# Remainder differences made once on the compact channels and transposed by DMA, in place of subtractions of transposed remainder tiles, together with a new order of the work

## Chip, cores, metric

The kernel runs on one core of a Trainium2 chip. The metric is the device time of one execution in microseconds (us), lower is better. A profiled execution has its own "span", the time from the first to the last instruction, some 2 us shorter than the device time. All comparisons are between executions in the fast state, at a granted TensorE clock of 0.99 or more, but for one profile whose state is unknown, which is marked.

Engines are named as in the profile: PE is TensorE's matmuls, PEld its weight loads, DVE is VectorE, ACT is ScalarE, POOL is GpSimd, SP is SyncE. "L727" is a line of the kernel. The change moves the line numbers by two or so: the matmul helper is L727 before and L729 after.

## The reference

A causal convolution in time with 15 taps two steps apart, a gate, and a projection. x is (2, 16000, 144), w is (15, 144, 288), w_o is (144, 144), all bfloat16.

```python
h = sum over i of  xp[:, pad - 2*i : pad - 2*i + T, :] @ w[i]      # 15 taps, 288 columns
z = tanh(h[..., :144]) * sigmoid(h[..., 144:])
return z @ w_o
```

## The kernel before

The convolution isn't computed tap by tap. Time is dealt out in octets of eight steps to 128 rows, and a fast-convolution scheme builds sums of taps (weights) and differences of inputs (data). Fewer products are needed that way, and VectorE pays for it in subtractions. The 144 channels are split: 128 fill the contraction dimension of a matmul ("A": tiles XA, V, DU, DD, and GX, GV, GU, GD, which are differences of these), and the other 16 ("B", the remainder) are first packed, so that 8 time steps of 16 channels fill 128 rows.

B's way before the change: VectorE copies the 16 channels into XBc, four phases of time (step modulo 4). ScalarE copies a window of it into a staging tile STB, a DMA transposes STB into XB, and VectorE makes two difference tiles, BE and BF, from XB. The matmuls of one kind ("D groups") read BE and BF.

```python
def load_xb(o):                      # staging of the remainder of octet o
    ...
    for h in range(2):
        def cp(v, h=h):              # ScalarE, 4 blocks of 128 columns, 2 copies per octet
            src = bass.AP(XBc[:].tensor, (MB - 1 - m4 - h) * DB, [[4 * MB * DB, NP], [MB * DB, 4], [1, 128]])
            return v.activation(STB[:, q, 4 * h:4 * h + 4, :], src, ACT.Copy)
        g.add("act", cp, r=..., w=[("STB", q, h)], dur=0.5, prio=2, soft=gate[:1])
    g.add("sp", lambda e: e.dma_start_transpose(XB[:, s, :, :], STB[:, q, :, :]...), ...)

def b_diffs(o):                      # VectorE, 2 subtractions of 128x512 per octet, 30 octets
    s, p, q = bslot(o), bslot(o - 1), dslot(o)
    tt(ap(BE, 4 * q, [4]), ap(XB, 8 * s + 2, [(4, 2), 2]), ap(XB, 8 * s, [(4, 2), 2]), ...)
    tt(ap(BF, 4 * q, [4]), ap(XB, 8 * p + 6, ...), ap(XB, 8 * s, [(4, 2), 2]), ...)
```

STA and STB have two slots each (octet modulo 2), so a third octet's staging waits until the first one's transpose has landed.

The main loop runs 30 units. A unit is a list of items, given by a pattern string ("+" means that the item belongs to a later unit, so that work overlaps). The items that matter here: VE and VF make two partial sums in PSUM, the memory that TensorE writes its sums to; X0 and X1 make two more, which ScalarE copies to UX; the four D groups D11, D01, D00, D10 finish the four outputs; O items are the projection. VectorE adds the partial sums:

```python
PATTERN = "Y0a O2+ X0a+ O1+ Y0b X0b+ D11 D00 S0+ X1a+ D10 Y01 S1+ X1b+ D01 VE+ O0+ VF+"

# three per unit, "Xp sums" (Xp<-PS,UX, L1006): partial sum + UX into SBUF; a PSUM pair comes free
g.add("dve", ... wslot(wi), both(vb, 0, N2), UX[...], ALU.add ..., prio=1)
# three per unit, "PS+Xp sums" (PS<-PS,Xp, L1018): the Xp sum back into PSUM for D01, D00, D10
g.add("dve", ... both(d, 0, N2), src, wslot(wi), ALU.add ..., prio=0)
# one per unit, "PS+UX sum" (PS<-PS,UX, L1027): in place in PSUM, for D11
g.add("dve", ... both(vb, 0, N2), both(vb, 0, N2), UX[...], ALU.add ..., prio=0)
```

The order of every engine's instructions is fixed when the kernel is built. A list scheduler runs a rough model of the engines and always takes the instruction with the smallest `key = (st, op.prio, op.idx)`: earliest modelled start, then the lower priority number, then program order. Subtractions have priority 2. At run time each engine works its list off in that order.

## Time and profile before

The median was 327.86 us of three executions (327.82 to 328.47).

From the page of the kernel before: busy time of each engine (share of the span, number of instructions), the chain of waits by engine (the chain of work that ended last, followed back from the end), two groups of instructions (line, engine, operation, tiles, shape, count | busy us, mean ns | idle time before them and what ended it), and the remainder's transposes (count, median us from issue to landing).

```profile
PE 317.5 (97%) x2702; PEld 245.7 (75%) x2702; DVE 301.3 (92%) x659; ACT 261.5 (80%) x629; POOL 17.0 (5%) x29
...
PE 82%; DVE 13%; DMA 2%; ACT 1%; issue 1%; POOL 0%; POOLq 0%
...
L1006 DVE TENSOR_TENSOR Xp<-PS,UX 128x576 f32<-128x576 f32 x90 | 65.3, 752 | 6.4 <-PE PS L727 5.8
...
L655 ACT ACTIVATE STB<-XBc 128x512 bf16<-128x512 bf16 x60 | 35.7, 628 | 1.6 <-DVE XBc L535 1.1 <-DMA XB<-STB 0.4
...
XB<-STB SPq DMA_TRANSPOSE x30, 3.6
```

TensorE is the engine that ends last, 82% of the chain, and VectorE is nearly as busy. The Xp sums alone are 65.3 us of VectorE's time, with little idle time before them; the 60 BE and BF subtractions are 25 us of instruction time, 20 us from start to start.

A steady stretch of the kernel before, from the table by stretches (the columns are the stretch, its length, then busy us and instruction counts of PE, PEld, DVE, ACT, POOL, then the clock, the DMA share and GB/s):

```profile
120.00:160.00 40.00, 40.00 (x336) 30.69 (x335) 39.52 (x84) 34.16 (x84) 0.00 (x0) 1.00 0.76 163
```

VectorE works 39.52 of 40 us and TensorE starts 336 matmuls.

The largest wait of weight loads in the whole run before (engine, tile and line <- what ended the wait: us in total, times, longest):

```profile
PEld PS L727 <- DVE PS L1027: 5.0, 22, 0.2
```

It is one short wait in most units, for the PS+UX sum. Weight loads overlap matmuls, so only a part of it is lost time (1.94 of the 5.0 us, as worked out under the result).

VectorE's timeline in the kernel before, over part of one unit (start, duration, instruction; a note in brackets gives idle time before it, and its cause):

```profile
157.90 0.76 DVE L1006 TENSOR_TENSOR Xp<-PS,UX 128x576 f32<-128x576 f32 x1
158.57 0.30 DVE L756 TENSOR_TENSOR Z<-TS 128x288 bf16<-128x288 f16 x1
158.79 1.41 DVE L1006 TENSOR_TENSOR Xp<-PS,UX 128x576 f32<-128x576 f32 x2
160.12 0.68 DVE L673 TENSOR_TENSOR V<-XA 128x1024 bf16<-128x1024 bf16 x1
160.72 0.76 DVE L1027 TENSOR_TENSOR PS<-PS,UX 128x576 f32<-128x576 f32 x1
```

TensorE's weight loads in the kernel before at that moment:

```profile
161.53 0.24 PEld L727 LDWEIGHTS PS<-WA,DD 128*128 128x128 bf16 x3 [0.23 <-DVE PS L1027]
```

The PS+UX sum starts at 160.72. At 161.53 the first weight load of D11 (WA,DD) has waited for it.

### The profile page before, as it was taken

How to read it: one execution, taken by the hardware profiler on the slowest of the kernel's cores; microseconds unless marked ns; L12 is line 12 of the kernel's file. 1: busy time of each engine (PE TensorE's matmuls, PEld its weight loads, DVE VectorE, ACT ScalarE, POOL GpSimd, SP SyncE). 2: the span in 40 equal slices, each digit the busy share in tenths (PEclk: the TensorE clock that was granted, in tenths of full speed). 3: DMA queues.
4: the chain of work that ended last, by engine and by line, in shares of the span. 5: the costliest groups of instructions: out<-in, count | busy, mean ns of one | idle time of the engine just before them, and what ended most of it. 6: DMA issues, size and time to landing. Idle time of an engine off the chain costs nothing.

```text
span 325.7 us, 7051 instructions
## 1 busy us (share of the span) xinstructions
PE 317.5 (97%) x2702; PEld 245.7 (75%) x2702; DVE 301.3 (92%) x659; ACT 261.5 (80%) x629; POOL 17.0 (5%) x29
## 2 busy tenths in 40 slices
PE   7999999999999999999999999999999999999993
PEld 7877767777777777777777777777777777777773
DVE  1999999999999999999999999999999999895773
ACT  3657669889797988979798897979889797788774
POOL 8750000000000000000000000000000000000000
PEclk9999999999999999999999999999999999999998
DMA  8899975929386492939749193984929193321443
GB/s 211 275 115 241 178 161 51 247 49 203 114 175 174 93 239 49 201 117 177 174 91 254 35 192 125 121 228 84 252 47 205 39 183 93 74 73 38 109 111 109
DMA packets 112461, 46.46 MB, mean 143 GB/s; under 512 B 103774, under 2 KB 106255, under 8 KB 112429
## 3 DMA queue, kind: packets, MB, share of 16 engines
q1 hardware_dynamic: 111385, 45.54, 65.2%
q0 software_dynamic: 512, 0.33, 0.4%
q8 instruction: 21, 0.34, 0.4%
q10 hardware_dynamic: 532, 0.16, 0.2%
q14 instruction: 11, 0.09, 0.1%
HBM read 11.82 MB, written 9.22 MB: 65 GB/s over the span
## 4 chain that ended last, share of the span: by engine, by line
PE 82%; DVE 13%; DMA 2%; ACT 1%; issue 1%; POOL 0%; POOLq 0%
PE PS L727 72%; PE PS L826 8%; DVE Xp L1006 2%; DMA XA<-STA 2%; DVE V L673 2%; PE PS L541 1%; DVE PS L1018 1%; DVE DD L673 1%; DVE STA L636 1%; DVE DU L673 1%; DVE Z L756 1%; DVE GD L673 1%; DVE WC L616 1%; DVE GU L673 1%; DVE PS L1027 0%
## 5 line engine op out<-in xcount | busy, mean ns | idle before, releaser
L1006 DVE TENSOR_TENSOR Xp<-PS,UX 128x576 f32<-128x576 f32 x90 | 65.3, 752 | 6.4 <-PE PS L727 5.8
L1018 DVE TENSOR_TENSOR PS<-PS,Xp 128x576 f32<-128x576 f32 x90 | 68.2, 759 | 1.8 <-ACT OS L834 0.9
L727 PE MATMUL PS<-WA,GD 128*128 128x288 bf16 x360 | 69.8, 286 | 0.0
L748 ACT ACTIVATE TS<-PS 128x288 f16<-128x288 f32 x125 | 51.3, 410 | 17.0 <-PE PS L727 12.3
L885 ACT ACTIVATE PS<-PS 128x288 f32<-128x288 f32 x120 | 45.4, 402 | 16.1 <-PE PS L727 16.1
L751 ACT ACTIVATE TS<-PS 128x288 f16<-128x288 f32 x125 | 50.7, 406 | 0.0
L954 ACT ACTIVATE UX<-PS 128x576 f32<-128x576 f32 x60 | 39.0, 650 | 13.8 <-PE PS L727 12.5
L727 PE MATMUL PS<-WS,GU 128*128 128x288 bf16 x210 | 44.2, 286 | 0.0
L834 ACT ACTIVATE OS<-PS 128x432 bf16<-128x432 f32 (+1 forms) x88 | 42.4, 488 | 0.5
L826 PE MATMUL PS<-WOR,ZT 128*128 128x144 bf16 (+1 forms) x322 | 42.3, 253 | 0.0
L727 PEld LDWEIGHTS PS<-WA,GD 128*128 128x128 bf16 x360 | 34.1, 98 | 10.3 <-DVE PS L1018 0.6
L756 DVE TENSOR_TENSOR Z<-TS 128x288 bf16<-128x288 f16 x125 | 37.5, 301 | 3.9 <-ACT TS L751 3.8
L727 PE MATMUL PS<-WB,XB 128*128 128x288 bf16 x140 | 37.6, 286 | 0.0
L655 ACT ACTIVATE STB<-XBc 128x512 bf16<-128x512 bf16 x60 | 35.7, 628 | 1.6 <-DVE XBc L535 1.1
L727 PE MATMUL PS<-WB,BF 128*128 128x288 bf16 x120 | 34.3, 286 | 0.0
L727 PE MATMUL PS<-WB,BE 128*128 128x288 bf16 x120 | 34.3, 286 | 0.0
L826 PEld LDWEIGHTS PS<-WOR,ZT 128*128 128x128 bf16 x322 | 28.0, 98 | 6.1 <-ACT OS L834 0.6
L727 PE MATMUL PS<-WD,DD 128*128 128x288 bf16 x180 | 31.7, 286 | 0.3 <-ACT PS L885 0.2
L727 PE MATMUL PS<-WA,DD 128*128 128x288 bf16 x180 | 30.9, 287 | 0.0
L727 PE MATMUL PS<-WC,V 128*128 128x288 bf16 x180 | 30.6, 286 | 0.0
L727 PE MATMUL PS<-WT,DU 128*128 128x288 bf16 x120 | 24.8, 288 | 0.7 <-DVE Xp L1006 0.7
L727 PEld LDWEIGHTS PS<-WS,GU 128*128 128x128 bf16 x210 | 20.1, 98 | 6.1 <-ACT PS L885 0.6
(82 smaller groups left out, 513.2 us busy)
## 6 DMA issues: line engine op xcount, KB each, us to landing
Xr<-in_x_dram SPq DMA_DIRECT2D x15, 576.0 KB, 4.0
out_dram<-OS SPq DMA_DIRECT2D x30, 288.0 KB, 2.7
WA<-in_w_dram SPq DMA_DIRECT2D x3, 288.0 KB, 5.0
ZT<-Z SPq DMA_TRANSPOSE x32, 3.4
Xp<-in_x_dram SPq DMA_DIRECT2D x2, 252.0 KB, 4.8
XA<-STA SPq DMA_TRANSPOSE x30, 3.2
XB<-STB SPq DMA_TRANSPOSE x30, 3.6
Xp<-in_x_dram SPq DMA_DIRECT2D x1, 441.0 KB, 3.9
```

Of the source, the lines that this page charges most:

```text
L655: return v.activation(STB[:, q, 4 * h:4 * h + 4, :], src, ACT.Copy)
L673: return g.add("dve", lambda v: v.tensor_tensor(dst, a, b, ALU.subtract), r=r, w=wk, dur=t_tt(n), prio=prio, soft=gate[:1])
L727: return lambda t: t.matmul(bank(bk.b), lhsT=lhs(), rhs=rhs(), start=start, stop=True, skip_group_check=True)
L748: return a.activation(TS[:, s, 0, :, :], both(bk, 0, D), ACT.Tanh)
L751: return a.activation(TS[:, s, 1, :, :], both(bk, D, D), ACT.Sigmoid)
L756: return v.tensor_tensor(dst, TS[:, s, 0, :, :], TS[:, s, 1, :, :], ALU.mult)
L826: return t.matmul(PS[:, c0:c0 + n * D], lhsT=ZT[:, zt, blk, :], rhs=WOR[:, wi:wi + n, :].rearrange("p a b -> p (a b)"), start=first, stop= ...
L834: return e.tensor_copy(dst, src) if eng == "dve" else e.activation(dst, src, ACT.Copy)
L885: g.add("act", lambda e: e.activation(bank(bk.b + 1), bank(bk.b), ACT.Copy), w=[bk], dur=t_act(N2), prio=0)
L954: g.add("act", lambda e: e.activation(UX[:, k, u % NU, :, :], both(X, 0, N2), ACT.Copy), r=[X], w=[("UX", k, u % NU)], frees=[X], dur=t_ac ...
L1006: g.add("dve", lambda v, k=k, wi=wi, vb=vb, us=us: v.tensor_tensor(wslot(wi), both(vb, 0, N2), UX[:, k, us, :, :], ALU.add), r=[vb, ("UX", ...
L1018: return v.tensor_tensor(both(d, 0, N2), src, wslot(wi), ALU.add)
```

## The change

The difference of two time steps is the same whether it's taken before or after a transpose. The change takes it before: XBc grows to eight planes, VectorE subtracts once on the compact 16 channels (16 instructions in place of 60), and the differences travel through STB, the DMA and XB along with the sums' operands. STB and XB tiles grow from 8 to 12 blocks, so ScalarE copies and the DMA transposes half as much again. One difference has the opposite sign, hence a negated weight tile. Along with that, the XA tiles got 8 slots in place of 11, items were put in another order, the Xp sums got priority 0, staging is spread in smaller steps, and the last store goes out on SyncE's queue.

```diff
-    NA = 11
+    NA = 8
...
-    NB = 7
-    NBD = 4
+    NB = 6
-    PATTERNS = {29: "Y0a O2 O1 Y01 Y0b D11 D01 D00 D10 O0"}
-    SPREAS = 10
-    PATTERN = "Y0a O2+ X0a+ O1+ Y0b X0b+ D11 D00 S0+ X1a+ D10 Y01 S1+ X1b+ D01 VE+ O0+ VF+"
+    PATTERNS = {29: 'O2 O1 Y01 Y0a D11 O0 Y0b D01 D00 D10', 28: ..., 1: ..., 0: ..., 2: ...}
+    SPREAS = 9
+    PATTERN = "Y0a O2+ X0a+ O1+ Y0b X0b+ D11 D00 S0+ X1a+ D10 Y01 S1+ X1b+ D01 VE+ VF+ O0+"
...
-        XBc = sb("XBc", [NP, 4, MB, DB], BF16)
-        STB = sb("STB", [NP, NST, 8, 128], BF16)
-        XB = sb("XB", [NP, NB, 8, 128], BF16)
-        BE = sb("BE", [NP, NBD, 4, 128], BF16)
-        BF = sb("BF", [NP, NBD, 4, 128], BF16)
+        XBc = sb("XBc", [NP, 8, MB, DB], BF16)
+        STB = sb("STB", [NP, NST, 12, 128], BF16)
+        XB = sb("XB", [NP, NB, 12, 128], BF16)
...
+        def diff_b(eng, m0, nm, r, tag):
+            i0 = MB - m0 - nm
+            def f(v):
+                pat = lambda ph, grp: bass.AP(XBc[:].tensor, (ph * MB + i0) * DB, [[8 * MB * DB, NP], [grp, 2], [MB * DB, 2], [1, nm * DB]])
+                return v.tensor_tensor(pat(2, -2 * MB * DB), pat(6, -2 * MB * DB), pat(4, 2 * MB * DB + DB), ALU.subtract)
+            g.add(eng, f, r=r, w=[tag], dur=t_tt(4 * nm * DB), prio=2, soft=gate[:1])
...
-        def load_xb(o):
+        def load_xb(o, parts=(0, 1)):
...
-                    src = bass.AP(XBc[:].tensor, (MB - 1 - m4 - h) * DB, [[4 * MB * DB, NP], [MB * DB, 4], [1, 128]])
-                    return v.activation(STB[:, q, 4 * h:4 * h + 4, :], src, ACT.Copy)
+                    src = bass.AP(XBc[:].tensor, (MB - 1 - m4 - h) * DB, [[8 * MB * DB, NP], [MB * DB, 6], [1, 128]])
+                    return v.activation(STB[:, q, 6 * h:6 * h + 6, :], src, ACT.Copy)
...
-        def b_diffs(o):
-            ... (the two subtractions shown above)
...
-  (Xp sums)      ... dur=t_ps(2 * N2), prio=1)
+  (Xp sums)      ... dur=t_ps(2 * N2), prio=0)
...
-                fns += f + [mm(_Half(bk, h), lambda o=o: bt[:, dslot(o), 2 * (1 - k) + r, :], lambda: WB[:, j, :], False)]
+                fns += f + [mm(_Half(bk, h), lambda o=o: XB[:, bslot(o), 6 * (1 - k) + bi + r, :], lambda: WB[:, 0, :] if j == 0 else WC[:, 2, 3, :], False)]
...
-            return [lambda: fetch(o0), lambda: fetch(o1), pack, lambda: load_xa(o0), lambda: load_xa(o1), lambda: load_xb(o0), lambda: load_xb(o1)]
+            return [lambda: (fetch(o0), fetch(o1)), pack, lambda: load_xa(o0), lambda: load_xb(o0, (0,)), lambda: load_xb(o0, (1,)), lambda: load_xa(o1),
+                    lambda: load_xb(o1, (0,)), lambda: load_xb(o1, (1,))]
...
-        store_both("act", o0, o1, dls[2:], 4)
+        store_both("sp", o0, o1, dls[2:], 4)
```

More of the change, by code (lines that the diff above doesn't have):

```diff
@@ L370, in _conv_wavenet_kernel @@
     LAG = 2
-    PATTERNS = {29: "Y0a O2 O1 Y01 Y0b D11 D01 D00 D10 O0"}
+    PATTERNS = {29: 'O2 O1 Y01 Y0a D11 O0 Y0b D01 D00 D10', 28: 'Y0a X0a+ O1+ Y0b X0b+ O2+ D11 S0+ D10 X1a+ D00 Y01 S1+ X1b+ VE+ O0+ D01 VF+', 1: 'Y0a O2+ X0a+ Y0b X0b+ D11 X1a+ O1+ D00 S0+ D10 Y01 S1+ X1b+ D01 VE+ VF+ O0+', 0: 'Y0a X0a+ Y0b D11 X0b+ D00 X1a+ O2+ O1+ O0+ S0+ D10 Y01 S1+ X1b+ D01 VE+ VF+', 2: 'Y0a O2+ X0a+ O1+ Y0b X0b+ D11 D00 S0+ X1a+ D10 Y01 S1+ X1b+ D01 VE+ O0+ VF+'}
     SPREAD = 12
-    SPREAS = 10
-    PATTERN = "Y0a O2+ X0a+ O1+ Y0b X0b+ D11 D00 S0+ X1a+ D10 Y01 S1+ X1b+ D01 VE+ O0+ VF+"
+    SPREAS = 9
+    PATTERN = "Y0a O2+ X0a+ O1+ Y0b X0b+ D11 D00 S0+ X1a+ D10 Y01 S1+ X1b+ D01 VE+ VF+ O0+"
     with contextlib.ExitStack() as st:
@@ L388, in _conv_wavenet_kernel @@
         DD = sb("DD", [NP, ND, 2, 4, 128], BF16)
-        XB = sb("XB", [NP, NB, 8, 128], BF16)
-        BE = sb("BE", [NP, NBD, 4, 128], BF16)
-        BF = sb("BF", [NP, NBD, 4, 128], BF16)
-        WA = sb("WA", [NP, 16, N2], BF16)
+        XB = sb("XB", [NP, NB, 12, 128], BF16)
+        WA = sb("WA", [NP, 15, N2], BF16)
         WS = sb("WS", [NP, 8, N2], BF16)
@@ L452, in bslot @@
             return (o + 1) % NB
-        def dslot(o):
-            return (o + 1) % NBD
         def oct_of(e):
@@ L469, in win_b @@
             c4, m4 = (e + 2) % 4, (e + 2) // 4
-            return XBc[:, c4, MB - 1 - m4:MB - 1 - m4 + 8, :].rearrange("p m c -> p (m c)")
+            return XBc[:, 4 + c4, MB - 1 - m4:MB - 1 - m4 + 8, :].rearrange("p m c -> p (m c)")
         def dma(eng, out_fn, in_fn):
@@ L520, in _conv_wavenet_kernel @@
         g.add("pool", lambda p: p.memset(WB[:, 1, :], 0.0), w=[("WB", 1)], dur=0.3)
-        g.add("pool", lambda p: p.memset(XBc[:, 0:2, MB - 1, :], 0.0), w=["XBcz"], dur=0.2)
+        g.add("pool", lambda p: p.memset(XBc[:, 4:6, MB - 1, :], 0.0), w=["XBcz"], dur=0.2)
         g.add("pool", lambda p: p.memset(Z[:], 0.0), w=[("Z", i) for i in range(NZ)], dur=1.2)
@@ L531, in f @@
                 s = src.rearrange("p (m c) d -> p c m d", c=4)
-                dst = bass.AP(XBc[:].tensor, (MB - 1 - m0) * DB, [[4 * MB * DB, NP], [MB * DB, 4], [-DB, nm], [1, DB]])
+                dst = bass.AP(XBc[:].tensor, 4 * MB * DB + (MB - 1 - m0) * DB, [[8 * MB * DB, NP], [MB * DB, 4], [-DB, nm], [1, DB]])
                 if eng == "act":
@@ L550, in f2 @@
                     s = Xp[:, 0:2, DA:D]
-                    dst = bass.AP(XBc[:].tensor, 2 * MB * DB + (MB - 1) * DB, [[4 * MB * DB, NP], [MB * DB, 2], [1, DB]])
+                    dst = bass.AP(XBc[:].tensor, 6 * MB * DB + (MB - 1) * DB, [[8 * MB * DB, NP], [MB * DB, 2], [1, DB]])
                     return a.activation(dst, s, ACT.Copy)
@@ L588, in zf @@
             def zf(p, b_=b):
-                return p.memset(XBc[b_ * SEG:b_ * SEG + 1, :, MB - H // 4 - 1:MB, :], 0.0)
+                return p.memset(XBc[b_ * SEG:b_ * SEG + 1, 4:8, MB - H // 4 - 1:MB, :], 0.0)
             g.add("pool", zf, r=hk, w=hk + ["XBcz"], dur=0.35)
@@ L594, in fix @@
             s = Xp[:, H:E0, DA:D]
-            dst = bass.AP(XBc[:].tensor, 2 * MB * DB + (MB - 1 - H // 4) * DB, [[4 * MB * DB, NP], [MB * DB, 2], [1, DB]])
+            dst = bass.AP(XBc[:].tensor, 6 * MB * DB + (MB - 1 - H // 4) * DB, [[8 * MB * DB, NP], [MB * DB, 2], [1, DB]])
             return p.tensor_copy(dst, s)
@@ L612, in wev @@
         def wev(t, n):
-            return bass.AP(WA[:].tensor, t * N2, [[16 * N2, NP], [4 * N2, n], [1, N2]])
+            return bass.AP(WA[:].tensor, t * N2, [[15 * N2, NP], [4 * N2, n], [1, N2]])
         def wsum(dst, a, b, r, wk, dur, eng="dve"):
@@ L630, in compact_chunk, with diff_chunk @@
             cmp_op("dve", Xr[:, s, 0:c - a, DA:D], E0 + a, E0 + c, [("Xr", s)], ("XBc", ci), 0.16 + (c - a) * DB / 1900.0)
+        def diff_b(eng, m0, nm, r, tag):
[4 more added lines that the diff above has]
+            g.add(eng, f, r=r, w=[tag], dur=t_tt(4 * nm * DB), prio=2, soft=gate[:1])
+        def diff_chunk(ci):
+            a, c = CH[ci]
+            diff_b("dve", (E0 + a + 2) // 4, (c - a) // 4, [("XBc", ci), ("XBc", ci - 1)] if ci else [("XBc", 0)] + hk5, ("XBd", ci))
         def load_xa(o):
@@ L646, in load_xb @@
                 if e >= EP:
-                    ck.add(("XBc", chunk_of(e - E0)))
+                    ck.update([("XBc", chunk_of(e - E0)), ("XBd", chunk_of(e - E0))])
                 else:
-                    ck.update(hk5 + ["XBcz"])
+                    ck.update(hk5 + ["XBcz", "XBd_h"])
             m4 = (e0 + 2) // 4
-            for h in range(2):
+            for h in parts:
                 def cp(v, h=h):
-                    src = bass.AP(XBc[:].tensor, (MB - 1 - m4 - h) * DB, [[4 * MB * DB, NP], [MB * DB, 4], [1, 128]])
-                    return v.activation(STB[:, q, 4 * h:4 * h + 4, :], src, ACT.Copy)
-                g.add("act", cp, r=sorted(ck, key=str), w=[("STB", q, h)], dur=0.5, prio=2, soft=gate[:1])
+                    src = bass.AP(XBc[:].tensor, (MB - 1 - m4 - h) * DB, [[8 * MB * DB, NP], [MB * DB, 6], [1, 128]])
+                    return v.activation(STB[:, q, 6 * h:6 * h + 6, :], src, ACT.Copy)
+                g.add("act", cp, r=sorted(ck, key=str), w=[("STB", q, h)], dur=0.708, prio=2, soft=gate[:1])
+            if 1 not in parts:
+                return
             g.add("sp", lambda e: e.dma_start_transpose(XB[:, s, :, :], STB[:, q, :, :].rearrange("p a b -> p (a b)")),
-                  r=[("STB", q, 0), ("STB", q, 1)], w=[("XB", s)], dur=1.3, dma="xb", nbytes=8 * 128 * 128 * 2)
+                  r=[("STB", q, 0), ("STB", q, 1)], w=[("XB", s)], dur=1.7, dma="xb", nbytes=12 * 128 * 128 * 2)
         def xbk(o):
@@ L699, in v_third @@
                [("V", s, 0), ("V", p, 0), ("V", s, 1), ("V", p, 1)], [("DD", q)], 1024)
-        def b_diffs(o):
-            s, p, q = bslot(o), bslot(o - 1), dslot(o)
-            kb = xbk(o) + xbk(o - 1)
-            tt(ap(BE, 4 * q, [4]), ap(XB, 8 * s + 2, [(4, 2), 2]), ap(XB, 8 * s, [(4, 2), 2]), kb, [("BE", q)], 512)
-            tt(ap(BF, 4 * q, [4]), ap(XB, 8 * p + 6, [(8 * (s - p) - 4, 2), 2]), ap(XB, 8 * s, [(4, 2), 2]), kb, [("BF", q)], 512)
         def gslot(m):
@@ L802, in f @@
                 return e.dma_start(dst, src)
-            g.add(eng, f, r=[("OS", s, d) for d in dls for s in (s0, s1)], w=[], dur=0.6, dma="st" if eng == "sp" else "st2", nbytes=NP * n * D * 2)
+            g.add(eng, f, r=[("OS", s, d) for d in dls for s in (s0, s1)], w=[], dur=0.6, dma="st", nbytes=NP * n * D * 2)
         def ship(o, dls):
@@ L950, in item_Xb @@
                 f, kk = own(_Half(X, h), GU, "GU", m, 2 * k + r, h, XW[k])
-                fns += f + [mm(_Half(X, h), lambda o=o: XB[:, bslot(o), 4 * (1 - k) + r, :], lambda: WB[:, 2, :], False)]
+                fns += f + [mm(_Half(X, h), lambda o=o: XB[:, bslot(o), 6 * (1 - k) + 4 + r, :], lambda: WB[:, 2, :], False)]
                 keys += kk + xbk(o)
@@ L1006, in combine @@
                             g.add("dve", lambda v, k=k, wi=wi, vb=vb, us=us: v.tensor_tensor(wslot(wi), both(vb, 0, N2), UX[:, k, us, :, :], ALU.add),
-                                  r=[vb, ("UX", k, us)], w=[("W", wi)] + (xp_all if wn[0] <= NW else []), frees=[vb] if j == 0 else (), dur=t_ps(2 * N2), prio=1)
+                                  r=[vb, ("UX", k, us)], w=[("W", wi)] + (xp_all if wn[0] <= NW else []), frees=[vb] if j == 0 else (), dur=t_ps(2 * N2), prio=0)
                             if j == 0:
@@ L1037, in item_D @@
             aw = [(lambda i=4 * i + p: WA[:, i, :]) for i in range(4 if p < 3 else 3)]
-            bt, bkey = (BE, "BE") if j == 0 else (BF, "BF")
-            fns, keys = [], [("WB", j)] + wak
+            wb, bi = (0, 2) if j == 0 else (3, 0)
+            fns, keys = [], [("WB", wb)] + wak
             for h, o in ((0, o0), (1, o1)):
@@ L1045, in item_D @@
                     kk = [("DD", uslot(o - i)) for i in range(len(aw))]
-                fns += f + [mm(_Half(bk, h), lambda o=o: bt[:, dslot(o), 2 * (1 - k) + r, :], lambda: WB[:, j, :], False)]
-                keys += kk + [(bkey, dslot(o))]
+                fns += f + [mm(_Half(bk, h), lambda o=o: XB[:, bslot(o), 6 * (1 - k) + bi + r, :], lambda: WB[:, 0, :] if j == 0 else WC[:, 2, 3, :], False)]
+                keys += kk + xbk(o)
             g.add("pe", fns, r=keys, w=[bk], dur=len(fns) * MM)
@@ L1093, in _conv_wavenet_kernel @@
         compact_chunk(0)
+        g.add("act", lambda a: a.activation(WC[:, 2, 3, :], WB[:, 1, :], ACT.Copy, scale=-1.0), r=[("WB", 1)], w=[("WB", 3)], dur=0.31, prio=2)
+        diff_b("dve", 3, 7, hk5 + ["XBcz"], "XBd_h")
+        diff_chunk(0)
         load_xb(1)
@@ L1105, in _conv_wavenet_kernel @@
             n = 2 if i < 3 else 1
-            wsum(lambda i=i, n=n: WS[:, 2 * i:2 * i + n, :], lambda i=i, n=n: bass.AP(WA[:].tensor, 4 * i * N2, [[16 * N2, NP], [2 * N2, n], [1, N2]]),
-                 lambda i=i, n=n: bass.AP(WA[:].tensor, (4 * i + 1) * N2, [[16 * N2, NP], [2 * N2, n], [1, N2]]), [("WA", i)], [("WS", i)], 0.4 if n == 2 else 0.25)
+            wsum(lambda i=i, n=n: WS[:, 2 * i:2 * i + n, :], lambda i=i, n=n: bass.AP(WA[:].tensor, 4 * i * N2, [[15 * N2, NP], [2 * N2, n], [1, N2]]),
+                 lambda i=i, n=n: bass.AP(WA[:].tensor, (4 * i + 1) * N2, [[15 * N2, NP], [2 * N2, n], [1, N2]]), [("WA", i)], [("WS", i)], 0.4 if n == 2 else 0.25)
         wsum(lambda: WB[:, 2, :], lambda: WB[:, 0, :], lambda: WB[:, 1, :], [("WB", 0), ("WB", 1)], [("WB", 2)], 0.25)
@@ L1144, in prep @@
             v_third(o)
-            b_diffs(o)
         def stage(m):
@@ L1154, in pack @@
                     compact_chunk(nd[0])
+                    diff_chunk(nd[0])
                     nd[0] += 1
-            return [lambda: fetch(o0), lambda: fetch(o1), pack, lambda: load_xa(o0), lambda: load_xa(o1), lambda: load_xb(o0), lambda: load_xb(o1)]
+            return [lambda: (fetch(o0), fetch(o1)), pack, lambda: load_xa(o0), lambda: load_xb(o0, (0,)), lambda: load_xb(o0, (1,)), lambda: load_xa(o1),
+                    lambda: load_xb(o1, (0,)), lambda: load_xb(o1, (1,))]
         def prepare(m):
@@ L1162, in prepare @@
             return [lambda: v_first(o0), lambda: v_second(o0), lambda: v_first(o1), lambda: v_second(o1), lambda: g_diffs(m, ("GX",)),
-                    lambda: g_diffs(m, ("GU",)), lambda: v_third(o0), lambda: v_third(o1), lambda: g_diffs(m, ("GV",)), lambda: b_diffs(o0), lambda: b_diffs(o1),
+                    lambda: g_diffs(m, ("GU",)), lambda: v_third(o0), lambda: v_third(o1), lambda: g_diffs(m, ("GV",)),
                     lambda: g_diffs(m, ("GD",))]
@@ L1185, in _conv_wavenet_kernel @@
             if t % 2 and t >= -1:
-                todo_p, n_p, todo_s, n_s = prepare((t + 3) // 2), 12, stage((t + 5) // 2), 7
+                todo_p, n_p, todo_s, n_s = prepare((t + 3) // 2), 10, stage((t + 5) // 2), 8
                 step = 0
@@ L1240, in mksem @@
             return st.enter_context(nc.semaphore(name))
-        g.assign(mksem, {"xp": 8, "wa": 3, "wb": 2, "xr": NX, "xa": 4, "xb": 6, "zt": 3, "st": 6, "st2": 1, "wor": 16})
+        g.assign(mksem, {"xp": 8, "wa": 3, "wb": 2, "xr": NX, "xa": 4, "xb": 6, "zt": 3, "st": 6, "wor": 16})
         plan = g.plan_waits()
```

## The prediction

> What bounds it now. TensorE issues almost without a break. In the timeline, 288-column matmuls start 123 ns apart, which agrees with N/2.4 + 2.5 ns in the Trainium skill ("TensorE: Matmul & The Clock Gate", "Back-to-back issue gap": 122.5 ns). 2356 of these, 208 of 144 columns (62 ns) and 138 of 128 columns (56 ns) give an estimate of 310.5 us of pure issue in a span of 325.7 us. The chain of waits agrees: PE is 82% of it, from 55 to 315 us almost all of it. VectorE is nearly full too: in the table by stretches it is busy 39.5 of 40 us from 80 to 280 us, ScalarE 34.5. The chain lies on VectorE from 8 to 55 us.
>
> What TensorE loses beyond pure issue, read from gaps between matmul starts: 2.3 us before 10 us and 1.7 us before its first instruction (untouched); 2.0 us in the ramp from 20 to 60 us (waits for VectorE's Xp sums and a UX copy); about 2.9 us from 60 to 290 us, mostly each unit's first difference group waiting for VectorE's PS+UX sum (view of the waits: 5.0 us of weight-load idle, 22 times; some 0.09 us each is lost); 1.5 us from 290 us on; then 5 us of last evictions and stores.
>
> Removed: 60 VectorE subtractions of 128x512 (BE, BF), 419 ns long, 335 ns from start to start: 20 us. Added on VectorE: 16 subtractions on the compact channels, mostly 128x256, about 0.2 us each (estimate from 335 ns at 512 and 600 ns at 1024): 3 us. Net 17 us less, 301 to about 284 us; steady stretches 36.5 of 40.
> Added on ScalarE: the 60 STB copies grow from 512 to 768 columns; 628 ns becomes about 840 ns, at 0.83 ns an element (rate in the Trainium skill, "ScalarE: Activation LUTs", "What ACT_TABLE_LOAD costs"; this trace, 628 ns at 512 and 1018 at 1024, is close). That is 13 us more, 261 to 274 us, 36.5 of 40. Added on DMA: 30 XB transposes of 12 blocks in place of 8, +3.9 MB; landing 3.6 us becomes about 4.5, prefetched units ahead. TensorE's matmuls keep number and shape. Moved: patterns of the first, last and steady units, VF before projection O0, the last store to SyncE's queue, and both first XA transposes before the XB ones.
>
> On the critical path. Of 17 us only what TensorE waited for counts: most of the 2.9 us in the steady state (I expect 2.0), 1.0 of 2.0 in the ramp, 0.5 in the tail. Against it, ScalarE at 91% and heavier DMA in the ramp (already about full from 20 to 45 us) may cost 0.3. Sum: about 3.3 us. Predicted 324.5 us, range 321.8 to 327.6. Chances: faster by over 2% 0.05, within 2% 0.92, slower by over 2% 0.03.
>
> What would show it. Right: weight-load wait for the PS+UX sum gone, unit period from 9.485 us towards 9.40, VectorE near 284 us, ScalarE near 274, STB copies near 840 ns. Wrong: period unchanged, or new PE waits on ScalarE copies or XB transposes.
> What would make it wrong: ScalarE late with PSUM evictions; XB slots (6, now read until the last difference matmul) blocking the transposing queue; a DMA jam before 50 us; or the tail gaining over 1.5 us.

## The result

The kernel after took a median of 325.41 us (324.88 to 325.64, six executions); the kernel before, on the same chip and in the same rounds, 328.08 us (327.82 to 328.47, six executions). The ratio is 0.9916, with a 95% interval of 0.9904 to 0.9929. Ratios are quoted from the record, which takes fast executions of both kernels in the same rounds; they differ from a plain quotient of the quoted medians by up to 0.0006. The change is faster by 0.8%: within 2%, inside the predicted range, 0.9 us above the predicted 324.5.

The same lines of the page after the change:

```profile
PE 315.0 (97%) x2702; PEld 245.1 (76%) x2702; DVE 284.3 (88%) x616; ACT 265.3 (82%) x630; POOL 17.1 (5%) x29
...
PE 89%; ACT 4%; DVE 3%; DMA 2%; issue 1%; POOL 0%; ACTq 0%; POOLq 0%
...
L1008 DVE TENSOR_TENSOR Xp<-PS,UX 128x576 f32<-128x576 f32 x90 | 62.8, 750 | 20.4 <-PE PS L729 20.1
...
L661 ACT ACTIVATE STB<-XBc 128x768 bf16<-128x768 bf16 x60 | 50.5, 849 | 3.4 <-DMA XB<-STB 2.0
...
XB<-STB SPq DMA_TRANSPOSE x30, 4.8
```

VectorE lost 17 us and stands at the predicted 284. The idle time before the Xp sums rose from 6.4 to 20.4 us: a good part of the freed time reappears as VectorE waiting for TensorE. A copy into STB takes 849 ns instead of 628, as predicted, and a transpose lands after 4.8 us instead of 3.6. ScalarE's busy time rose by only 3.8 us, though its copies alone account for 50.5 − 35.7 = 14.8 us more. I had summed durations. By the instruction records, ScalarE's durations add up to 300.8 us before and 316.7 after, but neighbours overlap by 39.3 and 51.4 us. The Trainium skill ("ScalarE: Activation LUTs", "What ACT_TABLE_LOAD costs") gives 186 ns + 0.833 ns a column for such an instruction, from which 826 ns is an estimate at 768 columns, and says that back-to-back ones overlap by about 93 ns. This trace agrees with both, with 849 ns and about 0.1 us for each of some 490 adjacent pairs.

The steady stretch of the kernel after:

```profile
120.00:160.00 40.00, 40.00 (x341) 31.16 (x339) 37.03 (x77) 34.98 (x86) 0.00 (x0) 1.00 0.85 174
```

There are 341 matmuls in the 40 us in place of 336, at the same clock, with VectorE at 37.03.

Two of the weight-load waits of the whole run after:

```profile
PEld PS L729 <- ACT PS L914: 4.2, 23, 0.4
...
PEld PS L729 <- ACT UX L956: 1.3, 1, 1.3
```

The wait for the PS+UX sum (L1029 now) is gone. A new small one is there in most units, for a ScalarE copy of a PSUM pair (L914). The single wait for a UX copy lies in the ramp, which comes up below.

VectorE's timeline of the kernel after, over the matching part of a unit:

```profile
158.06 2.09 DVE L1008 TENSOR_TENSOR Xp<-PS,UX 128x576 f32<-128x576 f32 x3 [0.94 <-PE PS L729]
160.06 0.30 DVE L758 TENSOR_TENSOR Z<-TS 128x288 bf16<-128x288 f16 x1
160.28 0.76 DVE L1029 TENSOR_TENSOR PS<-PS,UX 128x576 f32<-128x576 f32 x1
160.94 0.68 DVE L681 TENSOR_TENSOR V<-XA 128x1024 bf16<-128x1024 bf16 x1
```

The three Xp sums run together, the PS+UX sum follows one gate product later, and the subtraction V now stands behind the sum. VectorE was idle for 0.94 us before them.

The repeating piece of the chain, in the kernel before:

```profile
150.90 6.96 PE PS L727 x56
...
160.38 6.96 PE PS L727 x56
```

And in the kernel after (the next such piece starts 9.37 us later, at 160.48):

```profile
141.74 7.89 PE PS L729 x64
151.11 7.89 PE PS L729 x64
```

### Where the time went, by stage

The first matmul of the GX group marks each unit well. From the starts of these matmuls in the traces (one profiled execution each):

```
                                     before    after    difference
start of unit 4                       69.83    71.05    +1.22   ramp
unit 4 to unit 28 (24 units)         228.38   225.79    -2.59   steady: 9.516 -> 9.408 us a unit
unit 28 to the last matmul            22.56    22.90    +0.34   tail
last matmul to the end                 4.94     4.09    -0.85   tail
span                                  325.7    323.8    -1.9
```

The steady state gained 2.6 us and the tail 0.5, and the ramp lost 1.2, in these two profiles.

Two things are not in this table. The time fell by more than the span: the medians by 2.7 us, the spans of these profiles by 1.9. Time less span is 1.7 to 1.9 us in every fast execution of a kernel with the new last store, and 1.7 to 2.4 us, with medians of 2.0 to 2.3 in all but one (e5, 1.8), in those with the old one, so some 0.3 to 0.4 us of the gain may lie outside the span. And single profiles stray: the profile before has a span of 325.7 us, where this kernel's median in the later rounds was 326.1 to 326.3; the profile after has 323.8, the longest of its six executions (323.1 to 323.8). With a typical 326.2 and 323.6, and steady state and tail as profiled, an estimate of the ramp's loss is 0.5 us and not 1.2.

For the steady state I also took each interval between matmul starts, less the undisturbed one (122.5, 62 or 55.5 ns for 288, 144 or 128 columns), and put the rest down to what the next weight load or matmul waited for. This is worked out from the trace, and is what "loss" means from here on ("excess" in the expectations is such a loss too, over the stretch that they name). The formula that the prediction cites stands in the Trainium skill ("TensorE: Matmul & The Clock Gate", "Back-to-back issue gap") as the gap of an isolated matmul, but this trace, with a median of 123 ns, agrees with it for 288 columns in a stream with weight loads:

```
loss over units 4 to 28, us   total   largest causes (times)
before                         4.21   PS+UX sum 1.94 (22); Xp sum, for a free PSUM pair 1.31 (23)
after                          1.62   ScalarE copy of a PSUM pair 0.72 (21)
```

So both of VectorE's waits vanished. Does that come from 17 us less work on VectorE, or from the order in which VectorE does the work?

### The profile page after: what moved, and what is told of

Its sections match the earlier page's. It is cut to its first block, busy times and chain, and to the rows that moved or that the text cites. A ratio compares the mean times of both kernels' runs of the same rounds, so it can differ in the third digit from the quotient of the medians.

```text
span 323.8 us, 7023 instructions
## 1 busy us (share of the span) xinstructions
PE 315.0 (97%) x2702; PEld 245.1 (76%) x2702; DVE 284.3 (88%) x616; ACT 265.3 (82%) x630; POOL 17.1 (5%) x29
## 4 chain that ended last, share of the span: by engine, by line
PE 89%; ACT 4%; DVE 3%; DMA 2%; issue 1%; POOL 0%; ACTq 0%; POOLq 0%
PE PS L729 77%; PE PS L828 9%; DMA XB<-STB 2%; ACT STB L661 2%; PE PS L535 1%; DVE WC L610 1%; ACT TS L750 1%; ACT TS L753 0%; ACT PS L887 0%; DVE V L681 0%; DVE WT L610 0%; DVE WD L610 0%; ACT XA L568 0%; PE PS L859 0%; PE PS L786 0%
## 5 line engine op out<-in xcount | busy, mean ns | idle before, releaser
L1008 DVE TENSOR_TENSOR Xp<-PS,UX 128x576 f32<-128x576 f32 x90 | 62.8, 750 | 20.4 <-PE PS L729 20.1
L729 PE MATMUL PS<-WB,XB 128*128 128x288 bf16 x260 | 71.9, 286 | 0.0
L661 ACT ACTIVATE STB<-XBc 128x768 bf16<-128x768 bf16 x60 | 50.5, 849 | 3.4 <-DMA XB<-STB 2.0
L753 ACT ACTIVATE TS<-PS 128x288 f16<-128x288 f32 x125 | 51.4, 411 | 0.0
L887 ACT ACTIVATE PS<-PS 128x288 f32<-128x288 f32 x120 | 46.1, 405 | 4.2 <-PE PS L729 4.1
L758 DVE TENSOR_TENSOR Z<-TS 128x288 bf16<-128x288 f16 x125 | 36.7, 298 | 4.5 <-ACT TS L753 4.2
L729 PE MATMUL PS<-WC,XB 128*128 128x288 bf16 x120 | 34.3, 286 | 0.0
L729 PEld LDWEIGHTS PS<-WB,XB 128*128 128x128 bf16 x260 | 25.4, 98 | 6.4
L729 PEld LDWEIGHTS PS<-WS,GU 128*128 128x128 bf16 x210 | 18.5, 98 | 7.5 <-ACT PS L887 0.3
```

The source lines that it names most:

```text
L661: return v.activation(STB[:, q, 6 * h:6 * h + 6, :], src, ACT.Copy)
L729: return lambda t: t.matmul(bank(bk.b), lhsT=lhs(), rhs=rhs(), start=start, stop=True, skip_group_check=True)
L753: return a.activation(TS[:, s, 1, :, :], both(bk, D, D), ACT.Sigmoid)
L758: return v.tensor_tensor(dst, TS[:, s, 0, :, :], TS[:, s, 1, :, :], ALU.mult)
L887: g.add("act", lambda e: e.activation(bank(bk.b + 1), bank(bk.b), ACT.Copy), w=[bk], dur=t_act(N2), prio=0)
L1008: g.add("dve", lambda v, k=k, wi=wi, vb=vb, us=us: v.tensor_tensor(wslot(wi), both(vb, 0, N2), UX[:, k, us, :, :], ALU.add), r=[vb, ("UX", ...
```

## The experiments

Two theories. L (load): VectorE was full, and taking 17 us off it lets the sums come in time. O (order): VectorE's place in the order decides, meaning what stands ahead of the sums in its queue; priority, pattern and staging did it, and the load matters little. All experiments but two give the right result. "Ratio" is against the kernel before in the same rounds.

### e1_orders_only

Before, with only the new order: patterns and priority.

```diff
-    PATTERNS = {29: ...}                     (old)
-    PATTERN = "... D01 VE+ O0+ VF+"
+    PATTERNS = {29: ..., 28: ..., 1: ..., 0: ..., 2: ...}   (as after)
+    PATTERN = "... D01 VE+ VF+ O0+"
-  (Xp sums)  prio=1
+  (Xp sums)  prio=0
```

> The kernel before, subtractions untouched, with the change's new orders of the work items and the new priority of the Xp sums alone. Theory L (VectorE's load was what made TensorE wait): VectorE stays near 301 us, the weight-load wait for the PS+UX sum stays near 5 us, the unit period stays near 9.485 us and the time near 328 us (0.5 either way). Theory O (the new order, with the VF group ahead of the projection, took the wait away): that wait goes under 1 us, the period falls to about 9.38 us, the time to about 325.5 us.

Measured: 331.42 us against 328.52, ratio 1.009 (1.0076 to 1.0105). It's slower, which neither theory had said. Two of the weight-load waits of this run:

```profile
PEld PS L727 <- ACT TS L751: 6.3, 11, 0.6
PEld PS L727 <- DVE PS L1018: 4.0, 13, 1.1
```

The wait for the PS+UX sum is gone, with VectorE's load as before: order alone removes it. But steady loss rose to 6.73 us, of which 4.74 is TensorE waiting, in 11 places, for the tanh and sigmoid evictions. In ScalarE's timeline three STB copies (0.6 us each, two of them back to back) stand shortly before those evictions, with a UX copy among them, in every second unit. The old way of staging puts both halves of an octet's copy into one step, and e5 below shows that the new order needs them apart. Unit 4 starts at 71.03 us here, as late as after, although the remainder tiles are the small ones.

### e2_subs_only

After, with only the old order: patterns and priority.

```diff
-    PATTERN = "... D01 VE+ VF+ O0+"   and the five special PATTERNS
+    PATTERN = "... D01 VE+ O0+ VF+"   and PATTERNS = {29: ...} of before
-  (Xp sums)  prio=0
+  (Xp sums)  prio=1
```

> The changed kernel with the orders of the work items and the priority of the Xp sums as before: the move of the subtractions alone. Theory L: VectorE near 284 us, the wait for the PS+UX sum gone, the period near 9.38 us, time 325 to 326 us. Theory O: the wait stays near 5 us, the period near 9.48 us, time about 328 us or more, since the ramp's loss of 1.3 us also stays.

Measured: 331.86 us against 328.52, ratio 1.0097 (1.0081 to 1.0113). VectorE is 16 us lighter, and the kernel is slower than the one before. The wait for the PS+UX sum is there as before (loss 2.01 us in 23 places), and a wait for the PS+Xp sums joins it (2.91 in 19). That speaks against L. Only the last store gained, since it's on SyncE's queue: 4.56 us from last matmul to end, against 4.94.

### e3_no_subs

Before, with BE and BF made only for the first octets. Later octets read old tiles: the result is wrong (relative error 0.43).

```diff
         def b_diffs(o):
+            if o > 4:
+                return
```

> The kernel before, which makes the BE and BF subtractions for the first four tiles only and then reads stale ones: a wrong result on purpose. VectorE loses some 17 us, ScalarE and the DMA get nothing added, the orders are the old ones. Theory L: the wait for the PS+UX sum goes, the period is near 9.38 us, the gap excess from 60 to 290 us falls from 2.9 to under 0.8 us, time about 325.3 us; the ramp stays as in the kernel before (2.0 us). Theory O: time about 328 us.

Measured: 328.1 us against 328.52, ratio 0.9992 (0.9976 to 1.0008). Nothing is gained. Its steady stretch, from the table by stretches:

```profile
120.00:160.00 40.00, 40.00 (x336) 30.86 (x335) 36.63 (x77) 34.85 (x85) 0.00 (x0) 1.00 0.75 157
```

Its largest weight-load wait (the edit moves L1027 to L1029):

```profile
PEld PS L729 <- DVE PS L1029: 5.1, 22, 0.2
```

And from its VectorE timeline:

```profile
159.69 0.76 DVE L1008 TENSOR_TENSOR Xp<-PS,UX 128x576 f32<-128x576 f32 x1 [0.54 <-PE PS L729]
...
160.57 1.42 DVE L1008 TENSOR_TENSOR Xp<-PS,UX 128x576 f32<-128x576 f32 x2
161.91 0.68 DVE L673 TENSOR_TENSOR V<-XA 128x1024 bf16<-128x1024 bf16 x1
162.51 0.76 DVE L1029 TENSOR_TENSOR PS<-PS,UX 128x576 f32<-128x576 f32 x1
```

VectorE is as light as after (36.63 of 40), yet TensorE starts 336 matmuls as before and waits 22 times as before. The freed time is spent idle, ahead of the first Xp sum, which waits for TensorE. After it come the same instructions in the same order, the V subtraction among them, and the PS+UX sum is just as late. This refutes L in the form I had predicted with, for the steady state. For the ramp the run says nothing: it keeps the eight BE and BF subtractions of the first four octets, from 30 to 45 us, and the first that it leaves out would come at about 60 us.

### e4_load_back

After, with as much VectorE work put back: two dummy subtractions of 128x512 for each octet, written to memory that is no longer used.

```diff
+        def dummy(o):                # two 128x512 subtractions of XB into a free part of Xp
+            ...
-                    ... lambda: g_diffs(m, ("GV",)),
+                    ... lambda: g_diffs(m, ("GV",)), lambda: dummy(o0), lambda: dummy(o1),
-                todo_p, n_p = prepare((t + 3) // 2), 10
+                todo_p, n_p = prepare((t + 3) // 2), 12
```

> The changed kernel with two dummy VectorE subtractions of 128x512 an octet put where the old ones stood, their result unused. VectorE near 303 us, all else as changed. Theory L: TensorE waits for VectorE again in each unit, period 9.45 us or more, time 327 to 329 us. Theory O: the order alone protects the first difference group: period 9.38 us, time about 325.4 us.

Measured: 326.79 us against 328.52, ratio 0.9947 (0.9935 to 0.996). Its steady stretch:

```profile
120.00:160.00 40.00, 40.00 (x341) 30.91 (x339) 40.00 (x88) 34.96 (x85) 0.00 (x0) 1.00 0.84 176
```

VectorE is busy all 40 of 40 us, fuller than in the kernel before, and TensorE starts 341 matmuls as in the kernel after. The steady period is 9.419 us a unit against 9.408. The 18 us of extra work cost about 1 us (0.9947 against 0.9916), of which the traces show 0.4 in the ramp and 0.3 in the steady state. With e3: in the steady state VectorE's load was not the cause.

### e5_orders_split and e6_split_only

e6 is before with the new staging alone: each STB copy is a step of its own. e5 is e6 with the new patterns and priority as well; it lacks the moved differences and the moved store.

```diff
-        def load_xb(o):
+        def load_xb(o, parts=(0, 1)):
...
-            return [fetch(o0), fetch(o1), pack, load_xa(o0), load_xa(o1), load_xb(o0), load_xb(o1)]
+            return [(fetch(o0), fetch(o1)), pack, load_xa(o0), load_xb(o0, (0,)), load_xb(o0, (1,)), load_xa(o1), load_xb(o1, (0,)), load_xb(o1, (1,))]
-    SPREAS = 10
+    SPREAS = 9
```

> The kernel before with its subtractions on VectorE, given the new orders and the change's spreading of the staging work (each of the two ScalarE copies of a tile its own step, eight steps in place of seven, nine for the spread). Theory S (the steady gain comes from the new orders together with the spread ScalarE copies; where the subtractions are made does not matter there): gap excess from 60 to 290 us under 0.8 us, unit period near 9.38 us, VectorE near 301 us; with the lighter ramp of the kernel before (about 2 us) the time is 324.5 to 326 us. Rival M (the moved subtractions are needed as well, VectorE at 301 us with real dependences blocks it): gap excess from 60 to 290 us 2 us or more, time 327 us or more.

> The kernel before with the spread staging alone, old orders and priority. Theory S: the wait for the PS+UX sum stays (about 5 us of weight-load idle, 22 times), excess from 60 to 290 us 2.5 us or more, time 327.5 to 329.5 us. If the spreading alone were what helps, the excess would be under 1 us and the time about 325.5 us.

Measured, against 328.2: e5 327.06, ratio 0.9966 (0.9951 to 0.998); e6 330.6, ratio 1.0072 (1.0057 to 1.0087). Split staging alone harms (an Xp sum that TensorE waits for grows from 1.31 to 3.49 us of loss). With the new orders it mends what e1 had broken: steady period 9.464 us, about half of the way from 9.516 to 9.408. What is left in e5 is a wait for the PS+Xp sums (1.39 us in 13 places) and one for an Xp sum (0.76 in 11). Loss from 60 to 290 us is 2.61 us, so M's expectation came and S's (under 0.8) didn't; e6 is slower than both had it. In 11 of the 13 places the PS+Xp sum that TensorE waits for stands directly behind BE and BF (1.23 of the 1.39 us). Moving the differences to the compact channels takes BE and BF out of there. e4 points to the place and not the time: it has the same orders and staging and as much VectorE work (nothing reads its dummies, though), but only one dummy stands directly before that PS+Xp sum, and TensorE doesn't wait for it; half of its dummies stand before the Xp sums, at 0.35 us of loss in two places. So the moved subtractions do count for much of the other half of the gain, by the places that they left. This is read from the timelines of kernels that also differ in tile size, and not tested alone.

### e11_prio_only

Before, with the priority of the Xp sums alone changed from 1 to 0.

```diff
-  (Xp sums)  prio=1
+  (Xp sums)  prio=0
```

> The kernel before with one number changed: the priority of the Xp sums, 1 to 0. All its subtractions stay on VectorE (about 301 us), patterns, staging and stores stay. The build shows the PS+UX sum directly behind the Xp sums on VectorE, nearly the same orders on TensorE and ScalarE. Theory Q: the waits for the PS+UX sum and for the Xp sums shrink from 3.3 us to under 1 us over the 24 steady units, unit period 9.38 to 9.45 us, time 325 to 326.5 us: as fast as the whole change. If the priority helps only together with the moved subtractions or the spread staging, the period stays at 9.5 us or more and the time at 328 us or more.

Measured: 326.99 us against 328.42, ratio 0.9962 (0.9946 to 0.9978). From its VectorE timeline:

```profile
155.23 0.42 DVE L673 TENSOR_TENSOR BE<-XB 128x512 bf16<-128x512 bf16 x1
155.57 0.76 DVE L1018 TENSOR_TENSOR PS<-PS,Xp 128x576 f32<-128x576 f32 x1
...
157.82 2.09 DVE L1006 TENSOR_TENSOR Xp<-PS,UX 128x576 f32<-128x576 f32 x3
...
160.04 0.76 DVE L1027 TENSOR_TENSOR PS<-PS,UX 128x576 f32<-128x576 f32 x1
160.71 0.68 DVE L673 TENSOR_TENSOR V<-XA 128x1024 bf16<-128x1024 bf16 x1
```

Its largest weight-load wait, and one case of it from the timeline of weight loads:

```profile
PEld PS L727 <- DVE PS L1018: 6.3, 27, 0.3
...
156.38 0.11 PEld L727 LDWEIGHTS PS<-WA,GD 128*128 128x128 bf16 x2 [0.26 <-DVE PS L1018]
```

One digit in the source turns the order to Xp sums, gate product, PS+UX sum, then V: the order of the kernel after. Both waits of the kernel before, 1.94 and 1.31 us of loss, are zero. But TensorE, no longer held there, now waits for PS+Xp sums, 2.14 us of loss in 23 places: 1.46 us in 12 where the sum stands directly behind BE and BF, and 0.55 us in 10 where it stands behind a DU subtraction and an STA copy. In the kernel before, the sum at 155.62 us stood behind the same BE subtraction and TensorE didn't wait for it. Net, a little over half of the steady gain (9.458 us a unit), and less than I had expected. Without the waits behind BE and BF 0.67 of the 2.14 us would be left, an estimate that no run tests: the new priority without BE and BF, and nothing else, was not built.

### e9_sum_prio_old

After, with that priority alone set back to 1. Built, it has the very order of the kernel after on TensorE and ScalarE; only VectorE's differs.

```diff
-  (Xp sums)  prio=0
+  (Xp sums)  prio=1
```

> The changed kernel with only the priority of the Xp sums as before. The build shows TensorE's and ScalarE's orders unchanged; on VectorE a gate product again stands between the first two Xp sums and a 0.6 us V or DD subtraction ahead of the PS+UX sum. Theory Q (what counts is what stands in VectorE's queue ahead of the sums that TensorE waits for, not how much VectorE has to do): the waits for the PS+UX sum and for the Xp sums come back, unit period 9.46 to 9.52 us against 9.41, time 326.6 to 328 us, VectorE's total unchanged at 284 us. If VectorE's total were what counts, nothing changes: 325.4 us.

Measured: 332.19 us against 327.98, ratio 1.0125 (1.0101 to 1.0149): slower than I had expected, and slower than the kernel before. Its weight-load waits:

```profile
PEld PS L729 <- DVE PS L1020: 6.3, 20, 0.7
PEld PS L729 <- DVE PS L1029: 5.5, 24, 0.2
```

And its VectorE timeline:

```profile
161.10 0.76 DVE L1008 TENSOR_TENSOR Xp<-PS,UX 128x576 f32<-128x576 f32 x1 [1.29 <-PE PS L729]
...
161.99 1.42 DVE L1008 TENSOR_TENSOR Xp<-PS,UX 128x576 f32<-128x576 f32 x2
163.32 0.68 DVE L681 TENSOR_TENSOR V<-XA 128x1024 bf16<-128x1024 bf16 x1
163.92 0.76 DVE L1029 TENSOR_TENSOR PS<-PS,UX 128x576 f32<-128x576 f32 x1
```

The old order is back (the gate product among the Xp sums, V before the PS+UX sum), and so is the wait, 5.5 us in 24 places against 5.0 in 22 before. VectorE stood idle for 1.29 us just before, so it has the time; what it has in its queue is in the wrong place. That the PS+Xp wait would come as well (2.92 us of loss) I had not expected.

### e10_vf_late

After, with the old steady pattern: VF after the projection again.

```diff
-    PATTERN = "... D01 VE+ VF+ O0+"
+    PATTERN = "... D01 VE+ O0+ VF+"
```

> The changed kernel with only the steady pattern as before (the VF group behind the projection O0), the priority of the Xp sums stays new. The PS+UX sum then starts about 0.25 us later but still directly behind the Xp sums. Theory Q: no wait for it returns, or one of under 0.03 us a unit: period 9.40 to 9.44 us, time 325 to 326.2 us. If VF's earlier place is what took the wait away, the period is 9.48 us or more and the time over 326.8 us.

Measured: 326.6 us against 327.98, ratio 0.9956 (0.9934 to 0.9977). The wait for the PS+UX sum doesn't come back, so VF's place is not what removed it. Another one appears:

```profile
PEld PS L828 <- ACT UX L956: 4.8, 23, 0.2
```

The projection's weight loads now stand behind a UX copy on ScalarE in 23 places (1.5 us of loss). The earlier VF is needed for that reason.

### e8_short_xb

After, with copies and transposes of 8 blocks, not 12, so wrong (relative error 0.33). It shows what the larger remainder tiles cost.

```diff
-                    src = ... [MB * DB, 6], [1, 128]])          -> STB[:, q, 6 * h:6 * h + 6, :]
+                    src = ... [MB * DB, 4], [1, 128]])          -> STB[:, q, 4 * h:4 * h + 4, :]
-            e.dma_start_transpose(XB[:, s, :, :], STB[:, q, :, :]...)
+            e.dma_start_transpose(XB[:, s, 0:8, :], STB[:, q, 0:8, :]...)
```

> The changed kernel with copies and transposes of 8 blocks in place of 12, read by the same matmuls: a wrong result on purpose. The orders and all of VectorE's work stay. If the 12-block tiles make the ramp worse (theory R), the excess from 20 to 60 us falls from 3.3 us to 2.3 us or less and ScalarE's wait for XB<-STB shrinks by over 1 us; the steady state stays as it is (excess under 0.5 us); time 324.2 to 325 us. If the ramp loss comes from the orders or the fewer XA slots, the excess stays at 3 us.

Measured: 324.15 us against 328.2, ratio 0.9872 (0.9859 to 0.9885). Against after's 0.9916 the larger tiles cost some 1.4 us: in the traces 0.9 in the steady state (9.369 us a unit; the wait for the ScalarE copy of a PSUM pair is gone, loss 0.69) and 0.4 in the ramp. I had expected that it would mend more of the ramp.

### e7_ramp_staging and e7b_look

After, with the first two octets that would need a second turn of the two staging slots staged elsewhere: in tiles (OS and Z) that are idle so early. No other octet changes.

```diff
+            if o in (3, 4):     # load_xa: stage in Z instead of STA
+                st2, sk = Z[:, o - 2, 0:1024], [("Z", o - 2, d) for d in range(8)]
...
+            if o in (3, 4):     # load_xb: stage in OS instead of STB
+                st2 = OS[:]...[:, (o - 3) * 1536:(o - 2) * 1536]
```

> The changed kernel, where tiles 3 and 4 are staged in the output and gate buffers, idle at that time, so that neither ScalarE's nor VectorE's copies wait there for an earlier transpose to land. Theory R (in the ramp the in-order engines stand behind a staging copy that waits for a transpose, which the bigger XB transposes delay): the ScalarE idle of 2.0 us for XB<-STB and the VectorE idle of 1.1 us for XA<-STA go, the excess from 20 to 60 us falls from 3.3 us to about 1.5 us, time 323.5 to 324.5 us, faster than both kernels. If the ramp is limited by the transposes' own bytes instead, the excess stays above 2.5 us and the time near 325.4 us.

> The same kernel as the ramp staging run, for a profile, since that run's profile fell in an execution with a clock of 0.559. Expected: no ScalarE idle for XB<-STB and no VectorE idle for XA<-STA from 20 to 60 us, gap excess there about 2.0 to 2.5 us against 3.3 us (the timed runs were about 1 us faster than the changed kernel), steady period 9.41 us as in the changed kernel.

Measured: 324.53 us (three fast executions, 324.49 to 324.57) against 328.2, ratio 0.9886 (0.9872 to 0.99). A fourth, the profiled one, took 552.83 us at a granted clock of 0.559; it's left out, and nothing here tells why it happened. The second look at the same kernel gave 323.94 us and a usable profile (span 322.1 us, clock state unknown for a single execution, but the fast executions had spans of 322.7 and 322.8). So this version beats both kernels.

From the chain of waits of the kernel after, in the ramp:

```profile
19.56 6.65 DMA XB<-STB
26.24 1.58 ACT STB L661 x2
...
30.79 8.27 PE PS L729 x66
```

From the chain of this kernel in the same time:

```profile
17.94 9.74 PE PS L736 x78
...
29.14 9.74 PE PS L736 x78
```

In the kernel after, the chain runs over a transpose that takes 6.65 us from the last copy to landing, then over ScalarE, which had stood 1.97 us idle before the next STB copies for want of a free slot, and which does four of them before the UX copy that TensorE waits for at 30.7. With other slots the chain stays mostly on TensorE (85% of it from 18 to 45 us, against 46%). Unit 4 starts at 69.40 us here, against 71.05 after and 69.83 before. Loss from 12 us to unit 4: 2.13 us here, 3.58 after, 2.22 before. By cause, the loss for the UX copy is 1.17 us after and 0.42 here, as before, and that for a DU tile, which is made from XA, 0.86 and 0.16: in these profiles both staging tiles count. This kernel has 8 XA slots too, so they alone don't explain the longer ramp of the kernel after. Single profiles stray (this one's span is 0.6 us under that of the fast executions): by the ratios (0.9886 against 0.9916) the edit is worth 1.0 us of time, by these two profiles 1.7.

Summary of what the runs say, with ratios against before. The last two columns are from one profile each; the start of unit 4 strays with it (e3's profiled execution was 1.2 us above the median of its runs, e5's 0.8, e4's 0.6 below):

```
                                         ratio    us per steady unit   start of unit 4
before                                     -            9.516               69.83
after                                    0.9916         9.408               71.05
e1 new orders only                       1.009          9.621               71.03
e2 old orders, differences moved         1.0097         9.654               71.52
e3 before, without the subtractions      0.9992         9.515               71.62
e4 after, VectorE load put back          0.9947         9.419               71.48
e5 new orders + split staging            0.9966         9.464               71.07
e6 split staging only                    1.0072         9.608               70.56
e7 after, ramp staged elsewhere          0.9886         9.407               69.40  (e7b)
e8 after, short remainder tiles          0.9872         9.369               70.69
e9 after, old priority of Xp sums        1.0125         9.653               71.61
e10 after, old steady pattern            0.9956         9.473               70.83
e11 before, new priority of Xp sums      0.9962         9.458               70.35
```

## Why the prediction was right or wrong

**The time (right).** 324.5 was predicted, with 321.8 to 327.6, and the same class; 325.41 was measured. In part this was luck: the steady term came out for another reason than predicted, the ramp term had the wrong sign, and they partly made up for each other. In the traces the terms are: steady −2.59, ramp +1.22 (by typical spans about +0.5), tail −0.51.

**The steady state (right in size, wrong in reason).** I had "2.0" of 2.9 us, and 2.6 came. The sign that I named, the weight-load wait for the PS+UX sum gone and the unit period near 9.40, came true. The reason that I gave was that "Of 17 us only what TensorE waited for counts", that is, that the freed VectorE time would pay the waits. The list of what moved doesn't name the new priority of the Xp sums at all. e3 took off the same load and changed nothing (0.9992; 22 waits as before). e4 put it back and kept the steady gain (9.419 us). What counts is what stands directly before the sums in VectorE's queue. The priority of the Xp sums removes both old waits at once (e11); spread staging and an earlier VF keep ScalarE from becoming the next wait (e1 against e5, e10); and the moved subtractions leave the places before the PS+Xp sums (e11 and e5 against e4 and after, by reading only). Each piece alone gives a little over half of it at best, or harms (e1, e2, e6), so they don't add up.

**The ramp (wrong, also in sign).** I had "1.0 of 2.0 in the ramp" as a gain, since the chain of the kernel before lies on VectorE there. Unit 4 starts 1.22 us later instead (about 0.5 by typical spans). Whether VectorE's lighter ramp is worth anything was not tested alone: e3 keeps the ramp's subtractions. With the staging mended (e7) the ratio of 0.9886 is 3.7 us of time; less the steady state, the tail and 0.35 outside the span, about 0.3 is left for a ramp shorter than before, an estimate that would be a part of the predicted 1.0. In the kernel after, larger transposes and only two staging slots hold up ScalarE's copies, and ScalarE, in order, holds up the evictions behind them. Taking that wait away (e7) takes 1.0 us off by the ratios and 1.65 by the profiles, so most or all of the loss. Short tiles alone take off 0.4 (e8). The larger tiles are not the only way to lose it: e1 and e5 have the small tiles with the new orders, and unit 4 starts at 71.03 and 71.07 us. Their loss from 12 us on is 3.73 and 3.01 us, with 0.42 for the UX copy as before, and more for VectorE's GU and PS+Xp (2.0 and 1.5 us together). So what the new orders cost in the ramp, and what the slots, isn't separated. I had named a DMA jam before 50 us as a risk, but charged only 0.3 us for it and ScalarE together.

**Cost of the larger tiles (too low).** "ScalarE at 91% and heavier DMA in the ramp ... may cost 0.3": e8 puts it at some 1.4 us, 0.9 of them in the steady state, where TensorE waits for a ScalarE copy.

**ScalarE's load (wrong).** 274 us were predicted and 265.3 measured, since I had added up durations. The copies' own duration was right (840 predicted, 849 ns measured), and overlap took most of the rest.

**The rest.** VectorE at 284 us: right. Landing of the XB transposes "about 4.5": 4.8. Tail "0.5": 0.51. Two more readings split the tail: e1 has the new tail order with the old store and took 27.37 us from unit 28 to the end, e2 the old order with the new store, 27.12, against 27.50 before and 26.99 after. So about 0.4 us comes from the store's queue and 0.1 from the order.

**What stays open.** Why split staging alone makes the Xp sums late (e6) was not followed up, nor, by a run of its own, what part of the ramp's loss e7 takes from the XA and what from the XB slots, and what the new orders alone cost in the ramp. The part of the moved subtractions in the steady gain is a difference of two kernels that also differ in tile size.

## What to carry to other kernels

When an engine works off a fixed order, ask for each wait which instruction stands directly before the one that is waited for, and whether it could stand behind it; the engine's busy share doesn't tell that, and an engine at 100% can be harmless (e4, 40.00 of 40 us) while one with idle time is late (e9, 1.29 us idle just before). Test a "load" theory by taking the load away with a wrong result before building the right version of it: e3 took two lines, and would have shown that the subtractions' time was worth nothing in the steady state (0.9992). Then look again: when a wait goes, the next place in the queue can start to hold (e11: PS+Xp sums behind BE, 1.46 us of loss, where the kernel before lost 0.05). In a ramp, count the staging slots: when a transfer grows, an in-order engine that waits for a free slot delays everything behind it, and two more slots for the first round bought 1.0 us here (ratio from 0.9916 to 0.9886).

## What the Trainium skill lacked or had wrong

- "Perfetto Trace Analysis", "Identifying the Most-Contended Engine", says to use occupancy for Vector, Scalar and GPSIMD, and "Optimize this engine first". By that measure VectorE, 39.52 of 40 us busy, was next in line. Taking its load off to 36.63 of 40 us gave a ratio of 0.9992 (e3), and filling it to 40.00 of 40 left the steady gain in place (e4, 9.419 us a unit). The section lacks the step from occupancy to the place in the in-order queue: one priority number, without any change of load, gave 0.9962 (e11) and 1.0125 (e9).
- "Perfetto Trace Analysis", "Tensor Engine Instruction (MATMUL, LD_WEIGHTS)", says in passing that ScalarE and VectorE are strict FIFO. What that costs, it doesn't say: 1.97 us of ScalarE idle before an STB copy in the ramp, and a kernel 1.0 us slower by the ratios than with free slots (e7).
- "DMA: Bandwidth & Descriptors", "Latency and other measured facts", has a bandwidth for transposes by DMA, 261 GB/s, but no time to landing. The only duration of such a transfer that I found in the skill is 1309 ns for a single 128x128 tile ("VectorE: DVE Perf Modes", "The three transpose paths"); none for larger ones. Here a transpose of 8 such tiles (256 KB) landed after a median of 3.2 us (XA) and 3.6 us (XB) before the change, one of 12 (384 KB) after 4.8 us; in the ramp, with others on the same queue, the chain shows 6.65 us. No run here isolates the rate.
